# An earlier first transfer, and a last V pair cut into smaller transfers, in a transfer-bound decode kernel

## The chip, the cores and the metric

The kernel runs on one core of a Trainium2 chip. The metric is the time of one execution on the device, in microseconds (us). It is read from several executions of each kernel, alternated on the same chip. The engines carry the names of the profiles: PE does the matmuls, DVE is the vector engine, ACT the scalar engine, POOL the general-purpose one, and SP only issues transfers. L429 is line 429 of the kernel.

## The reference

One new token for each of four sequences attends over a long K/V cache; a gated MLP of the same input is mixed in.

```python
B, D, H, Sk, Dh, F = 4, 1024, 32, 8192, 128, 3584      # all bfloat16
def reference(A_x, A_k_cache, A_v_cache, A_wq, A_wo, B_x, B_w_r, B_w_gate, B_w_up, B_w_down, gate_w):
    x = A_x
    g = sigmoid((x * gate_w).sum(-1, keepdims=True))
    q = heads(x @ wq)                                    # (B, H, 1, Dh)
    p = softmax(einsum("bhqd,bhkd->bhqk", q, k_cache) * Dh ** -0.5)
    a = merge(einsum("bhqk,bhkd->bhqd", p, v_cache)) @ wo
    b = x + sigmoid(x @ w_r) * ((silu(x @ w_gate) * (x @ w_up)) @ w_down)   # B_ref runs on x, one token
    return g * a + (1 - g) * b
```

The two caches are 268 MB each and the weights bring the total to 576 MB. All of it has to be read once. (Totals and GB/s count in powers of ten; the sizes of single transfers below, 8 MB, 4 MB, 1 MB, are in units of 2^20 bytes.)

## The kernel before

All large transfers are issued by SP, in one order, into a ring of five slots of 4 MB. A "pair" is 8 MB: four heads of K or of V, filling two slots. There are 32 K pairs and 32 V pairs. A K pair goes through DVE, which transposes it piece by piece into one of two T buffers, and then through PE. A V pair goes to PE directly: 64 matmuls in 8 chunks of 8.

```python
NS = 5                                                   # ring slots
ttp = ctx.enter_context(tc.tile_pool(name="ttp", bufs=2))    # the T buffers
...
def load_pair(src, n, apart=False):
    a = slots(2)
    if a + 1 < NS and not apart:
        nc.sync.dma_start(out=flat[:, lo:lo + 2 * n], in_=src)      # 8 MB at once
        ...
def k_pair(d):
    ks = load_pair(kv_view(A_k_cache, d), RING)
    for n in range(RD):                                  # 8 pieces
        T = ttp.tile([P, CJ, 2, 32, 2], BF, name="T", tag="T")
        nc.vector.transpose(out=T..., in_=kn[...])
        for he in range(4):
            for z in range(2):
                nc.tensor.matmul(sps[:, z, :], lhsT=Z[:, he, s:s + P], rhs=T[...], ...)
        ...
def v_pair(d):
    if d < ND - 1:
        vs = load_pair(vv, RING, apart=d >= ND - 3)
    else:                                                # the last V pair
        vs = [ring[:, slots(1)] for _ in range(2)]
        nc.sync.dma_start(out=vs[0], in_=vv[:, 0:RING])              # 4 MB
        for c in range(4):                                           # 4 x 1 MB
            lo, hi = c * RING // 4, (c + 1) * RING // 4
            nc.sync.dma_start(out=vs[1][:, lo:hi], in_=vv[:, RING + lo:RING + hi])
    for c in range(RD):                                  # 8 chunks of 8 matmuls
        ...
```

The end of the program, in order: two wo blocks (1 MB each), the last V pair, the other six wo blocks (the last two in halves). The last 32 matmuls need the finished attention rows.

```python
    if (kind, d) == ("v", ND - 1):
        for g in range(2):
            wo_block(g)()
    ...
    last = [wo_block(g) for g in range(2, NWB - 2)]
    last += [wo_block(g, r, r + FR // 2) for g in (NWB - 2, NWB - 1) for r in (0, FR // 2)]
    last.pop(0)(); flush(); flush_late(); last.pop(0)()
    o_rows(GE, NWB)
    for use in last:
        use()                                            # the last 32 matmuls
```

Of the kernel before, what the change touches and what calls it, by code (L numbers as in the profile page):

```python
# [18 lines left out]
def keep_weights(nc):  # L19

    for f in nc.m.functions:
        for block in f.blocks:
            held, kept, alone = None, [], False
            for i in block.instructions:
                if i.engine == mybir.EngineType.PE:
                    if isinstance(i, mybir.InstLdweights):
                        a, y = i.ins[0], i.sync_info
                        key = (a.memref, a.offset, str(a.ap), str(a.dtype), i.tile_size, i.tile_position, i.is_transpose)
                        free = y is None or not (y.on_wait or y.on_update)
                        if free and held == key:  # L30
                            continue
                        held = key
                    elif not isinstance(i, mybir.InstMatmult) or i.ldweights is not False:
                        held = None
                kept.append(i)
            block.instructions = kept


@with_exitstack
def kernel(  # L40
# [15 lines left out]
    nc = tc.nc  # L56
# [19 lines left out]
    RING = JR * Dh  # L76
# [13 lines left out]
    mps = ctx.enter_context(tc.tile_pool(name="mps", bufs=2, space=PSUM))  # L90
    ctx.enter_context(tc.manual_schedule(engines={mybir.EngineType.PE, mybir.EngineType.DVE, mybir.EngineType.Pool}))
    nc.at_finalize(keep_weights)

    ring = const.tile([P, NS, RING], BF, name="ring")
    turn = [0]

    def slots(n):
        at = turn[0]
        turn[0] = (at + n) % NS
        return at  # L100
# [3 lines left out]
# [4 lines that stand above are left out]
            lo = a * RING  # L108
            nc.sync.dma_start(out=flat[:, lo:lo + 2 * n], in_=src)  # L109
            return [flat[:, lo:lo + n], flat[:, lo + n:lo + 2 * n]]  # L110
        halves = [ring[:, a], ring[:, (a + 1) % NS]]
        for i, half in enumerate(halves):
            nc.sync.dma_start(out=half[:, 0:n], in_=src[:, i * n:(i + 1) * n])
        return halves

    def small(shape, dtype=F32):
        return mps.tile(shape, dtype, name="small", tag="small")
# [27 lines left out]
    for he in range(4):  # L145
        half, e = divmod(he, 2)
# [170 lines left out]
    def flush():  # L317
        while pending:
            pending.pop(0)()

    def flush_late():
        while late:
            late.pop(0)()

    def heads(d):
        return divmod(d * NQ, H)

    def kv_view(cache, d):
        b, h0 = heads(d)
        return cache[b, h0:h0 + NQ].rearrange("h (r j) d -> (h r) (j d)", j=2 * JR)  # L330
# [77 lines left out]
    def v_pair(d):  # L408
        b, h0 = heads(d)
        g, t = divmod(d, GD)  # L410
        row = NM * t
        B_ = PB[g % 2]
        vv = kv_view(A_v_cache, d)
        if d < ND - 1:
            vs = load_pair(vv, RING, apart=d >= ND - 3)
        else:
            vs = [ring[:, slots(1)] for _ in range(2)]
            nc.sync.dma_start(out=vs[0], in_=vv[:, 0:RING])
            for c in range(4):
                lo, hi = c * RING // 4, (c + 1) * RING // 4  # L420
                nc.sync.dma_start(out=vs[1][:, lo:hi], in_=vv[:, RING + lo:RING + hi])
        n = 0
        for c in range(RD):
            vn = vs[c // JT]
            for z in range(2):
                for w in range(2):
                    for e in range(2):
                        j0 = CJ * (c % JT) + 16 * z + 8 * w + 4 * e
                        nc.tensor.matmul(o_ps[row:row + NM, e, :],  # L429
                                         lhsT=B_[:, RD * t + c, z, w].rearrange("p e s j -> p (e s j)"),  # L430
                                         rhs=vn[:, j0 * Dh:(j0 + 4) * Dh], start=(n == 0), stop=(n == 4 * RD - 1),
                                         skip_group_check=True)
                    n += 1
                    if n == 4:
                        flush()
                    if n == 16:
                        flush_late()
        if t < GD - 1:
            return
        o_sb = OS  # L440
        nc.scalar.activation(out=o_sb[:], in_=o_ps[:, 0, :], func=ACT.Copy, scale=mE[:, 0:1])  # L441
        nc.vector.scalar_tensor_tensor(out=o_sb[:], in0=o_ps[:, 1, :], scalar=mE[:, 1:2], in1=o_sb[:],  # L442
                                       op0=ALU.mult, op1=ALU.add)

        def finish():
            oT = small([P, GH])
            for q in range(4):
                nc.tensor.matmul(oT[:, :], lhsT=o_sb[:, q * Dh:(q + 1) * Dh],  # L448
                                 rhs=selg[:, q].rearrange("p t s -> p (t s)"), start=(q == 0), stop=(q == 3))

            def scaled():
                hg = h0 + NQ - GH
                nc.vector.scalar_tensor_tensor(out=OT[:, hg:hg + GH, b], in0=oT[:, :], scalar=sgb[:, 1, b:b + 1],
                                               in1=rinv_t[g][:], op0=ALU.mult, op1=ALU.mult)
            late.append(scaled)
        pending.append(finish)
# [12 lines left out]
    for kind, d in order:  # L469
        if kind == "k":  # L470
            k_pair(d)
            if d in side:
                side[d]()
# [3 lines that stand above are left out]
        if kind == "v":  # L477
            v_pair(d)
        if (kind, d) == ("k", ND // 2):
            add_x()  # L480
        if (kind, d) == ("v", ND - 2):
            o_rows(0, GE)
# [44 lines left out]
```

## Time and profile before

| before | value | read from |
|---|---|---|
| time, three executions | 1345.84, 1345.85, 1346.68 us | runs |
| span of the trace | 1345.3 us (execution of 1347.05 us) | page |
| share of the DMA engines, queue q1 | 99.3% | page |
| PE, DVE busy | 78%, 46% | page |
| last PE wait for V | 1.86 us | PE timeline |

These lines are from the page of the kernel before: the span, the granted TensorE clock in tenths, the DMA share in tenths and the rate in 40 slices, and the queue with packets, megabytes and share.

```profile
span 1345.3 us, 7987 instructions
...
PEclk9787988988998888899898889898899798989999
DMA  9999999999999999999999999999999999999997
GB/s 413 427 436 427 442 429 425 443 431 419 443 435 419 437 435 433 433 433 430 435 435 435 435 431 431 427 428 434 435 423 442 433 419 431 431 427 440 426 426 318
...
q1 hardware_dynamic: 13976, 575.68, 99.3%
```

The transfers fill the span: no slice but the last is below 413 GB/s. So a microsecond can be had at the two ends.

This is the end of the chain of waits of the kernel before (start, duration, what):

```profile
...
1283.83 32.50 DMA ring<-in_A_v_cache_dram
1316.38 13.11 PE o_ps L429 x60
1331.11 0.76 DVE OS L442
1331.91 1.07 PE small L448 x8
1332.98 1.82 PE acc L192 x8
1335.32 7.08 PE acc L192 x32
```

The transfer of the 4 MB half of V releases PE at 1316.38 us. From there to the end the chain is PE with its small steps on DVE (the step on ACT is among the lines left out), and no transfer.

The SP timeline of the kernel before shows issues (start, duration, what). The semaphore records of the trace count SP's landings on eight semaphores in turn, 16 increments for a transfer. From 1301.67 to 1326.34 us each of the eight issues comes 0.02 to 0.07 us after the last increment for the transfer eight issues before it. That makes an issue time a landing time:

```profile
0.80 0.40 SPq L109 DMA_DIRECT2D ring<-in_A_wq_dram  x1
...
1306.69 0.33 SPq L301 DMA_DIRECT2D ring<-in_A_wo_dram  x1
1316.40 0.33 SPq L301 DMA_DIRECT2D ring<-in_A_wo_dram  x1
1326.34 0.33 SPq L301 DMA_DIRECT2D ring<-in_A_wo_dram  x1
```

The first line is the first transfer of the program. The three others give the landings of the wo block just ahead of the last V pair (1306.69), of the 4 MB half (1316.40) and of the last 1 MB quarter of V (1326.34).

The PE timeline of the kernel before around the same place (start, duration, engine, line, operation, out<-in, elements, count, then in brackets the idle time before and what ended it):

```profile
1301.69 7.89 PE L429 MATMUL o_ps<-ring,PB 128*32 128x512 bf16 x28 [2.69 <-DMA ring<-in_A_v_cache_dram]
...
1310.90 3.62 PE L192 MATMUL acc<-ring,LT 128*4 128x512 bf16 x16 [0.32 <-DVE LT L291]
1316.38 13.11 PE L429 MATMUL o_ps<-ring,PB 128*32 128x512 bf16 x60 [1.86 <-DMA ring<-in_A_v_cache_dram]
```

The first line, the second half of the pair before the last, has 28 matmuls in 7.89 us. Here a part of it ran at half clock, and the clock record has 0.5 for 3.41 us from 1302.25 us on.

### The profile page before, as it was taken

Reading aid. Unit: us, or ns where it says so; the run is one execution under the profiler, and the core shown is the slowest. Engines: PE = TensorE matmul, PEld = TensorE weight load, DVE = VectorE, ACT = ScalarE, POOL = GpSimd, SP = SyncE. Lnnn points to the kernel's source line nnn. Section 1 sums busy time; section 2 is a strip of 40 time slices with the busy share of each in tenths; the row PEclk is TensorE's granted clock in tenths of the full one; section 3 lists DMA queues with packets and bytes.
Section 4 is the critical chain, followed back from the end, with each engine's and each line's share of the span. In section 5 each row is a group of like instructions: output and inputs, shape, how many; then the busy total and the mean of one; then the engine's idle time right before and its main releaser. Section 6 shows DMA issues by size and latency. Waiting matters only on the chain.

```text
span 1345.3 us, 7987 instructions
## 1 busy us (share of the span) xinstructions
PE 1050.1 (78%) x4536; PEld 229.2 (17%) x2348; DVE 623.1 (46%) x358; ACT 51.4 (4%) x46; POOL 59.0 (4%) x91
## 2 busy tenths in 40 slices
PE   2565977777887778878977779697779679877888
PEld 0111111112111111111211111111111112111211
DVE  4465655534445553345455456146555254556000
ACT  0000100001000100001000010001000010000000
POOL 4000100001000100001000010000000010000000
PEclk9787988988998888899898889898899798989999
DMA  9999999999999999999999999999999999999997
GB/s 413 427 436 427 442 429 425 443 431 419 443 435 419 437 435 433 433 433 430 435 435 435 435 431 431 427 428 434 435 423 442 433 419 431 431 427 440 426 426 318
DMA packets 14031, 576.20 MB, mean 428 GB/s; under 512 B 1566, under 2 KB 1574, under 8 KB 2092
## 3 DMA queue, kind: packets, MB, share of 16 engines
q1 hardware_dynamic: 13976, 575.68, 99.3%
q8 instruction: 27, 0.44, 0.1%
q14 instruction: 8, 0.07, 0.0%
q10 hardware_dynamic: 20, 0.02, 0.0%
HBM read 575.68 MB, written 0.01 MB: 428 GB/s over the span
## 4 chain that ended last, share of the span: by engine, by line
DMA 58%; PE 23%; DVE 10%; issue 8%; ACT 0%; DVEq 0%; SPq 0%; POOL 0%
DMA ring<-in_A_k_cache_dram 50%; PE S_ps L358 11%; PE o_ps L429 11%; DVE T L352 10%; DMA ring<-in_A_v_cache_dram 5%; DMA ring<-in_B_w_gate_dram 3%; PE small L448 1%; PE acc L192 1%; PE o_ps L226 0%; ACT OS L441 0%; DVEq L352 0%; DVE OS L442 0%; ACT res L495 0%; SPq L109 0%; POOL Z L335 0%
## 5 line engine op out<-in xcount | busy, mean ns | idle before, releaser
L352 DVE STREAM_TRANSPOSE T<-ring 128x2048 uint32<-128x2048 uint32 x256 | 570.6, 2282 | 501.4 <-DMA ring<-in_A_k_cache_dram 425.9
L358 PE MATMUL S_ps<-T,Z 128*128 128x512 bf16 x2048 | 536.7, 410 | 220.8 <-DVE T L352 214.8
L429 PE MATMUL o_ps<-ring,PB 128*32 128x512 bf16 x2048 | 460.5, 387 | 37.6 <-DMA ring<-in_A_v_cache_dram 37.6
L358 PEld LDWEIGHTS <-Z 128*128 128x128 bf16 x1024 | 106.2, 104 | 643.6 <-issue 635.8
L429 PEld LDWEIGHTS <-PB 128*32 128x32 bf16 x1024 | 100.7, 99 | 395.2 <-issue 373.1
L383 ACT ACTIVATE PTs<-S_ps,negm 128x1024 bf16<-128x1024 f32 x8 | 8.9, 1114 | 994.7 <-DVE negm L380 994.7
L335 POOL TENSOR_TENSOR Z<-qa,mq 128x16 bf16<-128x16 bf16 x32 | 8.3, 262 | 808.4 <-PE S_ps L358 737.3
L442 DVE SCALAR_TENSOR_TENSOR OS<-o_ps,mE,OS 128x512 f32<-128x512 f32 x8 | 6.0, 751 | 68.8 <-ACT OS L441 68.8
L394 POOL COPY PB<-PT 32x1024 bf16<-32x1024 bf16 x16 | 30.4, 1897 | 26.8 <-DVE rex L396 26.5
L392 ACT COPY PB<-PT 32x1024 bf16<-32x1024 bf16 x16 | 30.6, 1914 | 10.7 <-DVE PT L385 10.6
L291 DVE CAST LT<-small 128x64 bf16<-128x64 f32 x2 | 0.4, 224 | 46.3 <-PE small L289 46.3
L376 POOL PARTITION_ALL_REDUCE gmx<-mex x8 | 3.2, 396 | 340.6 <-DVE mex L373 340.6
L371 DVE TENSOR_REDUCE m<-S_ps 128x1 f32<-128x1024 f32 x8 | 9.8, 1225 | 15.9 <-PE S_ps L358 15.9
L402 DVE RECIPROCAL rinv<-tot 128x16 f32<-128x16 f32 x8 | 2.0, 248 | 31.1 <-POOL tot L398 31.1
L385 DVE STREAM_TRANSPOSE PT<-PTs 128x1024 bf16<-128x1024 bf16 x8 | 10.0, 1245 | 12.1 <-ACT PTs L383 12.1
L192 PE MATMUL acc<-ring,LT 128*4 128x512 bf16 x64 | 14.5, 379 | 0.7 <-DVE LT L291 0.7
L139 PE MATMUL small<-identb,x 6*128 6x6 bf16 x8 | 0.6, 196 | 15.8 <-DMA x<-in_gate_w_dram 15.8
L448 PEld LDWEIGHTS small<-selg,OS 128*128 128x128 f32 x64 | 11.8, 260 | 7.0 <-issue 4.9
L192 PE MATMUL acc<-ring,hT 128*4 128x512 bf16 x56 | 12.2, 379 | 0.0
L448 PE MATMUL small<-selg,OS 128*128 128x16 f32 x64 | 10.6, 302 | 0.9 <-DVE OS L442 0.9
L226 PE MATMUL o_ps<-ring,xw 128*4 128x512 bf16 x56 | 4.9, 481 | 7.1 <-DMA ring<-in_B_w_gate_dram 7.1
L441 ACT ACTIVATE OS<-o_ps,mE 128x512 f32<-128x512 f32 x8 | 5.5, 687 | 120.2 <-PE o_ps L429 120.2
(71 smaller groups left out, 82.2 us busy)
## 6 DMA issues: line engine op xcount, KB each, us to landing
ring<-in_A_v_cache_dram SPq DMA_DIRECT2D x15, 4096.0 KB, 30.1
ring<-in_A_k_cache_dram SPq DMA_DIRECT2D x14, 4096.0 KB, 31.8
ring<-in_B_w_gate_dram SPq DMA_DIRECT2D x1, 7168.0 KB
ring<-in_B_w_up_dram SPq DMA_DIRECT2D x1, 7168.0 KB
ring<-in_B_w_down_dram SPq DMA_DIRECT2D x2, 3584.0 KB
ring<-in_A_wo_dram SPq DMA_DIRECT2D x6, 1024.0 KB, 27.0
ring<-in_A_v_cache_dram SPq DMA_DIRECT2D x4, 1024.0 KB, 34.0
ring<-in_A_wo_dram SPq DMA_DIRECT2D x4, 512.0 KB, 17.3
```

Of the source, the lines that this page charges most:

```text
L192: nc.tensor.matmul(out_ap, lhsT=lhsT, rhs=rhs, start=start, stop=True, skip_group_check=True)
L335: nc.gpsimd.tensor_tensor(out=Z[:, :, QP - 1:QP - 1 + P].rearrange("p e (q c) -> p e q c", c=QP)[:, :, :, 0], in0=qa[:, :, h0:h0 + NQ, b], ...
L352: nc.vector.transpose(out=T[:].rearrange("p j h i e -> p (j h i e)").bitcast(U32), in_=kn[:, c * CJ * Dh:(c + 1) * CJ * Dh].bitcast(U32))
L358: nc.tensor.matmul(sps[:, z, :], lhsT=Z[:, he, s:s + P], rhs=T[:, 16 * z:16 * z + 16, half, :, e], start=(t == 0 and n == 0 and he == 0), ...
L371: nc.vector.tensor_reduce(out=m1[:], in_=sps[:].rearrange("p z n -> p (z n)"), axis=AX.X, op=ALU.max)
L383: nc.scalar.activation(out=PTs[:], in_=sps[:].rearrange("p z n -> p (z n)"), func=ACT.Exp, bias=negm[:, 0:1], scale=scale, accum_out=rs[:, ...
L385: nc.vector.transpose(out=PT[:].rearrange("p j i -> p (j i)"), in_=PTs[:])
L392: nc.scalar.copy(out=Bv[at, :, :, q, :], in_=Pv[at])
L394: nc.gpsimd.tensor_copy(out=Bv[at, :, :, q, :], in_=Pv[at])
L429: nc.tensor.matmul(o_ps[row:row + NM, e, :], lhsT=B_[:, RD * t + c, z, w].rearrange("p e s j -> p (e s j)"), rhs=vn[:, j0 * Dh:(j0 + 4) * ...
L442: nc.vector.scalar_tensor_tensor(out=o_sb[:], in0=o_ps[:, 1, :], scalar=mE[:, 1:2], in1=o_sb[:], op0=ALU.mult, op1=ALU.add)
L448: nc.tensor.matmul(oT[:, :], lhsT=o_sb[:, q * Dh:(q + 1) * Dh], rhs=selg[:, q].rearrange("p t s -> p (t s)"), start=(q == 0), stop=(q == 3))
```

## The change

The intent is twofold. First, the first transfer of the program is moved ahead of the drain with which SP enters the barrier at the start (the trace of the kernel before has 0.7 us of waiting for SP there). Second, the first 4 MB half of the last V pair arrives as two transfers of 2 MB, so that PE can start on it about 5 us sooner.

```diff
+def begin_early(nc):
+    for f in nc.m.functions:
+        head = list(f.blocks[0].instructions)
+        ...
+        at = [n for n, i in enumerate(head) if i.engine == SP and isinstance(i, mybir.InstDrain)]
+        for block in f.blocks[1:2]:
+            body = list(block.instructions)
+            n = next(n for n, i in enumerate(body) if i.engine == SP and isinstance(i, mybir.InstDMACopy))
+            i = body[n]
+            if at and not (i.sync_info is not None and i.sync_info.on_wait):
+                block.instructions = body[:n] + body[n + 1:]
+                f.blocks[0].instructions = head[:at[0]] + [i] + head[at[0]:]
...
     nc.at_finalize(keep_weights)
+    nc.at_finalize(begin_early)
...
             vs = [ring[:, slots(1)] for _ in range(2)]
-            nc.sync.dma_start(out=vs[0], in_=vv[:, 0:RING])
-            for c in range(4):
-                lo, hi = c * RING // 4, (c + 1) * RING // 4
-                nc.sync.dma_start(out=vs[1][:, lo:hi], in_=vv[:, RING + lo:RING + hi])
+            for half, cuts in ((0, 2), (1, 4)):
+                for c in range(cuts):
+                    lo, hi = c * RING // cuts, (c + 1) * RING // cuts
+                    nc.sync.dma_start(out=vs[half][:, lo:hi], in_=vv[:, half * RING + lo:half * RING + hi])
```

(`SP` stands for the full name of the engine; the first cut skips a function that has transfers in its head already.)

More of the change, by code (lines that the diff above doesn't have):

```diff
@@ L36, in keep_weights @@
             block.instructions = kept
+def begin_early(nc):
+    for f in nc.m.functions:
+        head = list(f.blocks[0].instructions)
+        if any(isinstance(i, mybir.InstDMACopy) for i in head):
+            continue
+        at = [n for n, i in enumerate(head) if i.engine == mybir.EngineType.SP and isinstance(i, mybir.InstDrain)]
+        for block in f.blocks[1:2]:
+            body = list(block.instructions)
+            n = next(n for n, i in enumerate(body) if i.engine == mybir.EngineType.SP and isinstance(i, mybir.InstDMACopy))
+            i = body[n]
+            if at and not (i.sync_info is not None and i.sync_info.on_wait):
+                block.instructions = body[:n] + body[n + 1:]
+                f.blocks[0].instructions = head[:at[0]] + [i] + head[at[0]:]
 @with_exitstack
```

## The prediction

> **What bounds the kernel now.** The transfers. The page gives queue q1 99.3% of the 16 DMA engines' span and 428 GB/s; its 40 slices show none under 413 GB/s but the last (318). PE is busy 78%, DVE 46%. A microsecond counts only at the two ends: before the first byte and after the last.
>
> **Start.** The timeline shows the first SP transfer (8 MB of wq) issued at 0.80 us; fine windows show DMA traffic from about 1.5 us. The waits of the SP queue show 0.7 us in the entry barrier. The built program has the transfer before SP's drain, so it should be issued 0.5 to 0.7 us sooner. The queue never runs dry afterwards, so all later landings move by that much. PE gets wq at 23.21 us after idling 0.56 us; nothing at the start should eat the gain.
>
> **End.** Landings can be read from the SP timeline, because each late issue waits for an older landing: the 4 MB half at 1316.40, its quarters at 1318.88, 1321.37, 1323.85, 1326.3 us. PE waits 1.86 us for the half (chain of waits: 60 matmuls from 1316.38), then runs without a real gap: 64 matmuls to 1330.2, eviction and small steps, then 32 output matmuls from 1335.32 at 0.216 us each, to 1342.2; the span ends at 1345.3.
> With the half cut in two, its first 2 MB should land near 1311.5, before PE is free (1314.4). The PE wait vanishes; PE then stays just behind the landings (last quarter 1326.3, PE reaches it at 1326.5). PE alone would finish 1.9 us earlier, near 1340.3.
> But the last half-MB of wo is nearly as late. Fine windows show the DMA share falling from 1.05 at 1335.5 to 0.06 (one engine of 16) at 1339, and that engine moving data until 1340.65. [...] one straggler sets the landing. The four matmuls that need it started at about 1341.36, so only 0.6 us of slack exists. Of the 1.9 us about 0.5 is usable; the rest becomes a new PE wait for wo, about 1.3 us.
>
> **Added cost.** One more transfer. 4 MB as one took 1316.40 - 1306.69 = 9.71 us, as four 9.94: about 0.08 us per extra transfer, on the path now. The last quarter's issue now waits for the landing of the pair before (1301.67 instead of 1291.96 us), with 9 MB still queued: harmless.
>
> **Sum.** -0.6 (start) -0.5 (end) +0.08 = -1.0 us: 1345.85 to 1344.8 us. 8 in 10: 1343.5 to 1346.1. Over 2% faster: 0.003; within: 0.994; slower: 0.003.
>
> **Signs.** Right: first SP issue at 0.0 to 0.3 us; wq matmuls about 0.6 us earlier; no wait of the V matmuls at the last pair's start; V done near 1327.6; a wait of about a microsecond before the last wo matmuls, released by a transfer; the last matmul 0.9 to 1.3 us earlier.
> Wrong at the start: same first issue, or earlier issue but unchanged first landing. Wrong at the end: last matmul 1.9 us or more earlier, or V matmuls still waiting.
>
> **What would make it wrong.** [...] the measured time starting at the first transfer, hiding the start's gain; half-rate matmuls, as at 1302 to 1305, in the last pair.

No term of the sum is cut: -0.6 -0.5 +0.08 = -1.0 us.

## The result, and the profile after

| kernel | executions | median | range | mean |
|---|---|---|---|---|
| before | 4 | 1346.26 us | 1345.84 to 1348.10 | 1346.62 |
| after | 4 | 1346.58 us | 1346.17 to 1347.79 | 1346.78 |

The ratio is 1.0001, with a 95% interval of 0.9984 to 1.0019. Ratios here are the mean time of one kernel's runs over that of the other's of the same rounds, so not quite the ratio of the medians that are quoted. The median lies above the predicted range of 1343.5 to 1346.1 us. The profiled executions differ a little: 1347.05 us before and 1346.29 us after, spans 1345.3 and 1344.6 us.

The end of the chain of waits of the changed kernel:

```profile
...
1270.46 30.53 DMA ring<-in_A_v_cache_dram
1301.06 24.63 DMA ring<-in_A_v_cache_dram
1325.75 14.89 DMA ring<-in_A_wo_dram
1340.68 1.04 PE acc L210 x4
1341.74 0.58 ACT res L513
```

The chain now ends in transfers: the last V quarter, then 14.89 us of wo, then the last four matmuls. In the kernel before it ended in PE.

The SP timeline of the changed kernel:

```profile
0.00 0.40 SPq L127 DMA_DIRECT2D ring<-in_A_wq_dram  x1
...
1305.95 0.33 SPq L319 DMA_DIRECT2D ring<-in_A_wo_dram  x1
1310.90 0.33 SPq L319 DMA_DIRECT2D ring<-in_A_wo_dram  x1
1315.80 0.33 SPq L319 DMA_DIRECT2D ring<-in_A_wo_dram  x1
1325.75 0.33 SPq L319 DMA_DIRECT2D ring<-in_A_wo_dram  x1
```

The first issue is at 0.00 us instead of 0.80 us. The first 2 MB landed at 1310.90 us, the second at 1315.80 us, the last quarter of V at 1325.75 us: 0.59 us sooner than before. The prediction's terms (0.6 us for the start less 0.08 us for the extra transfer) give 0.52 us; with the 0.80 us that the issue moved they would give 0.72 us.

The PE timeline of the changed kernel at the end:

```profile
...
1312.62 0.39 PE L447 MATMUL o_ps<-ring,PB 128*32 128x512 bf16 x1
...
1313.50 11.63 PE L447 MATMUL o_ps<-ring,PB 128*32 128x512 bf16 x52
1325.72 1.89 PE L447 MATMUL o_ps<-ring,PB 128*32 128x512 bf16 x8 [0.60 <-DMA ring<-in_A_v_cache_dram]
1328.21 1.89 PE L210 MATMUL acc<-ring,LT 128*4 128x512 bf16 x8 [0.60 <-DMA ring<-in_A_wo_dram]
...
1335.70 4.76 PE L210 MATMUL acc<-ring,LT 128*4 128x512 bf16 x20 [0.38 <-DMA ring<-in_A_wo_dram]
1340.68 1.02 PE L210 MATMUL acc<-ring,LT 128*4 128x512 bf16 x4 [0.22 <-DMA ring<-in_A_wo_dram]
```

The matmuls on the last V pair started at 1312.62 us, at first interleaved one by one with those on wo (in the lines left out), before the second 2 MB were there, as predicted. PE then caught up with the transfers and waited for them: 0.60 us, 0.38 us and 0.22 us are idle times put down to the landing of V or wo. The last four matmuls began at 1340.68 us, 0.68 us sooner than before (1341.36 us, worked out from the 32 matmuls of the chain: 1335.32 us plus 28 times 0.216 us).

### In the middle

Between the two ends something had changed that neither part of the change touches. These are the windows of the kernel before (columns: stretch, length, busy time and count of PE, weight loads, DVE, ACT, POOL, then the granted clock, DMA share and GB/s):

```profile
478.00:508.00 30.00, 22.70 (x98) 5.62 (x53) 18.78 (x10) 0.69 (x1) 0.52 (x2) 0.89 1.01 437
508.00:538.00 30.00, 23.37 (x94) 4.82 (x47) 13.19 (x6) 0.00 (x0) 0.00 (x0) 0.89 1.00 429
```

The same windows of the changed kernel:

```profile
478.00:508.00 30.00, 22.67 (x84) 5.83 (x45) 18.81 (x10) 0.69 (x1) 0.28 (x2) 0.83 1.00 424
508.00:538.00 30.00, 25.13 (x107) 5.34 (x53) 14.04 (x7) 0.00 (x0) 0.24 (x1) 0.94 0.98 422
```

From 478 to 508 us the changed kernel moved 424 GB/s instead of 437 GB/s, and its clock was 0.83 instead of 0.89. The PE timeline shows where. Before:

```profile
486.43 3.57 PE L358 MATMUL S_ps<-T,Z 128*128 128x512 bf16 x8 [5.46 <-DVE T L352]
489.80 1.00 PE L448 MATMUL small<-selg,OS 128*128 128x16 f32 x8
490.65 3.65 PE L358 MATMUL S_ps<-T,Z 128*128 128x512 bf16 x16
```

After:

```profile
486.29 3.57 PE L376 MATMUL S_ps<-T,Z 128*128 128x512 bf16 x8 [5.93 <-DVE T L370]
489.66 1.72 PE L466 MATMUL small<-selg,OS 128*128 128x16 f32 x8
491.22 5.79 PE L376 MATMUL S_ps<-T,Z 128*128 128x512 bf16 x16
```

The 16 matmuls that follow a wait took 5.79 us instead of 3.65 us. The clock record has 0.5 from 485.41 to 495.65 us, where that of the kernel before has it from 483.05 to 489.88 us. These matmuls are also what holds the two T buffers. DVE wants the next buffer and can't have it. The DVE timelines show it, that of the kernel before first, where four transposes follow each other without a wait:

```profile
492.58 8.89 DVE L352 STREAM_TRANSPOSE T<-ring 128x2048 uint32<-128x2048 uint32 x4
```

The changed kernel:

```profile
494.83 6.72 DVE L370 STREAM_TRANSPOSE T<-ring 128x2048 uint32<-128x2048 uint32 x3 [2.49 <-PE S_ps L376]
```

DVE lost 2.49 us there, so the last read of the K slot was late, so the transfer that refills the slot was issued at 497.17 us instead of 494.92 us, though the changed kernel had been ahead until then. The SP timelines, before and after:

```profile
494.92 0.33 SPq L109 DMA_DIRECT2D ring<-in_A_k_cache_dram  x1
```

```profile
497.17 0.33 SPq L127 DMA_DIRECT2D ring<-in_A_k_cache_dram  x1
```

The stream faltered by then. With the bytes of each packet spread over the packet's time, the changed kernel moved 369, 368 and 414 GB/s in the three stretches of 2 us from 498 to 504 us, where the kernel before moved 433 GB/s in each. The number of DMA engines with traffic fell to 14 or 15 of 16 from about 498.2 to 500.2 us, and 13 of the 50 packets of 64 KB that started between 495 and 503 us took 2.6 to 3.9 us, where all 57 of the kernel before took 2.4 us. Below, "runs dry" and "dry spell" mean such a dip of the rate. Why single packets got slower in it stays open.

I measured what such a spell costs from the transfer records, as the lead of the stream: the bytes moved by a time, divided by 428.6 kB per us, minus that time. Taken as an average from 460 to 490 us and again from 510 to 540 us, the lead rose by 0.49 us before (1.33 to 1.82 us) and fell by 0.19 us after (1.93 to 1.74 us). The changed kernel lost 0.68 us there, and that is as much as the start had given it: its lead over the kernel before was 0.60 us ahead of the place and -0.08 us behind it.

### The profile page after: what moved, and what is told of

It is laid out like the page before. It is cut to its first block, busy times and chain, and to the rows that moved or that the text cites. A ratio compares the mean times of both kernels' runs of the same rounds, so it can differ in the third digit from the quotient of the medians.

```text
span 1344.6 us, 7989 instructions
## 1 busy us (share of the span) xinstructions
PE 1050.9 (78%) x4536; PEld 229.7 (17%) x2348; DVE 620.5 (46%) x358; ACT 51.4 (4%) x46; POOL 57.7 (4%) x91
## 4 chain that ended last, share of the span: by engine, by line
DMA 63%; PE 19%; DVE 11%; issue 7%; another core or an unknown queue 0%; DVEq 0%; ACT 0%; SPq 0%
DMA ring<-in_A_k_cache_dram 52%; DVE T L370 11%; PE S_ps L376 11%; PE o_ps L447 8%; DMA ring<-in_A_v_cache_dram 7%; DMA ring<-in_B_w_gate_dram 3%; DMA ring<-in_A_wo_dram 1%; PE small L466 1%; DVEq L370 0%; PE acc L210 0%; ACT OS L459 0%; ACT res L513 0%; DVE rinv L420 0%; DVE OS L460 0%
## 5 line engine op out<-in xcount | busy, mean ns | idle before, releaser
L210 PE MATMUL acc<-ring,LT 128*4 128x512 bf16 x64 | 14.9, 378 | 2.0 <-DMA ring<-in_A_wo_dram 1.2
```

Source lines behind the costliest of these rows:

```text
L210: nc.tensor.matmul(out_ap, lhsT=lhsT, rhs=rhs, start=start, stop=True, skip_group_check=True)
```

## The experiments

The theories, by the letters that the expectations use:

- A: the change works as predicted, and only the scatter of executions hid it; the stream never runs dry.
- B: the gain of the start is lost in the middle of the stream.
- C (how B would come about): the stream runs dry when PE, at half clock, holds the two T buffers too long.
- D: the end of the kernel before is worse than its profile shows, because in most executions PE falls to half clock inside the last V pair.

The runs went in four batches, each on one chip, e1 to e4, e5 to e8, e9 to e12, e13 to e16, with the kernel before in each. The times of all (us):

| run | n | mean | median | standard deviation | before on the same chip, mean (n) | ratio, 95% |
|---|---|---|---|---|---|---|
| e1_both | 5 | 1346.44 | 1345.78 | 1.19 | 1347.97 (11) | 0.9987, 0.9975 to 0.9999 |
| e2_start | 6 | 1348.23 | 1347.95 | 2.1 | same | 0.9998, 0.9984 to 1.0012 |
| e3_end | 5 | 1346.46 | 1346.38 | 0.57 | same | 0.9987, 0.9975 to 0.9999 |
| e4_late | 5 | 1350.79 | 1350.16 | 1.07 | same | 1.0020, 1.0008 to 1.0031 |
| e5_t3_before | 5 | 1347.18 | 1346.61 | 1.34 | 1347.95 (9) | 0.9995, 0.9981 to 1.0008 |
| e6_t3_both | 5 | 1345.62 | 1345.62 | 0.47 | same | 0.9982, 0.9969 to 0.9996 |
| e7_before_short | 4 | 1347.93 | 1348.08 | 1.09 | same | 1.0000, 0.9986 to 1.0015 |
| e8_both_short | 4 | 1345.23 | 1345.34 | 0.58 | same | 0.9980, 0.9967 to 0.9994 |
| e9_warm_end | 5 | 1346.54 | 1346.51 | 0.38 | 1347.39 (9) | 0.9993, 0.9979 to 1.0006 |
| e10_warm_mid | 5 | 1345.93 | 1345.87 | 0.61 | same | 0.9988, 0.9975 to 1.0000 |
| e11_t3_warm_mid | 5 | 1345.57 | 1345.50 | 0.29 | same | 0.9985, 0.9973 to 0.9998 |
| e12_both_again | 5 | 1346.46 | 1346.32 | 1.42 | same | 0.9992, 0.9979 to 1.0005 |
| e13_warm_end_early | 5 | 1346.65 | 1346.45 | 0.83 | 1348.30 (9) | 0.9987, 0.9975 to 1.0000 |
| e14_t3_warm_late | 5 | 1345.82 | 1345.71 | 0.45 | same | 0.9980, 0.9966 to 0.9993 |
| e15_warm_end_again | 5 | 1346.57 | 1346.62 | 0.81 | same | 0.9987, 0.9974 to 0.9999 |
| e16_best_again | 5 | 1345.38 | 1345.59 | 0.58 | same | 0.9978, 0.9965 to 0.9990 |

### e1 to e4: the two parts apart, and a late start

e1_both is the changed kernel, unedited. e2_start and e3_end have one part each:

```diff
 # e2_start = before +
+    nc.at_finalize(begin_early)
 # e3_end = before +
+            for half, cuts in ((0, 2), (1, 4)): ...
 # e4_late = before, the first transfers made to wait for writes into their slots
+    nc.vector.memset(ring[:, 0, 0:8192], 0.0)
+    nc.vector.memset(ring[:, 2, 0:64], 0.0)
+    nc.vector.memset(ring[:, 4, 0:64], 0.0)
```

> The changed kernel again, beside the kernel before on one chip. Theory A (the change is worth about 0.7 us, the start's 0.8 us less a little at the end, and single executions scatter by more than that): mean 0.3 to 1.2 us below before, ratio 0.9991 to 0.9998, interval across 1; in the profile the last wo matmuls wait for a transfer again, and the last quarter of V lands 14.9 us before the last four matmuls. Theory B (what the start gains is lost again in the middle): the mean equals that of before to 0.3 us over all timed runs of this study, and the last landing is no earlier than before.

> Only the first transfer ahead of the entry barrier; the last V pair as before. Theory A: the first issue at 0.0 us instead of 0.8, the V matmuls of the last pair still wait about 1.9 us for their 4 MB, last matmuls end close behind the last landing; the time is 0.8 us below before (as e1 or 0.1 better), because the end of e1 is bound by the last landing anyway. If the end mattered as predicted, e1 would be 0.5 us faster than this one. Theory B: equal to before.

> Only the cut of the last V pair; the first transfer behind the barrier. Theory A: the V matmuls' 1.9 us wait goes, V is done 1.9 us sooner relative to the landing of the last quarter, but the last four matmuls wait for wo and start 14.9 us after the landing of the last quarter as before: -0.2 to +0.1 us. The prediction would have -0.4 us.

> The kernel before with a vector memset on the ring ahead of the first transfers, which delays the first issue by a time D read from the trace, about 4 us. Theory A: a shift of the first transfer passes to the end one for one, so the time is D above before, within 1 us. Theory B (a shift at the start is swallowed on the way): clearly less than D, under half of it.

By means, on one chip: before 1347.97, start alone 1348.23, end alone 1346.46, both 1346.44 us. The end is worth 1.5 to 1.8 us, three times what I had predicted, and the start nothing that these runs resolve. e4 issued its first transfer at 5.21 us, 4.41 us late, and took 2.8 us longer by the mean. That number fits neither A nor B. By the lead of the stream, e4 was 4.5 us behind the kernel before on average from 400 to 450 us and 4.0 us behind from 1250 to 1300 us, so most of a long delay at the start does reach the last transfers. (Both figures compare single profiles.) Why the mean of the times rose by less is open.

That the end is worth more than its profile said needed a reason. This is the PE timeline of e2_start, whose end is that of the kernel before:

```profile
1317.83 14.79 PE L447 MATMUL o_ps<-ring,PB 128*32 128x512 bf16 x60 [3.59 <-DMA ring<-in_A_v_cache_dram]
```

The wait is 3.59 us where the profile of before had 1.86 us, and the 60 matmuls took 14.79 us where they had taken 13.11 us. The granted clock of e2 was 0.50 from 1318 to 1320 us and 0.69 to 1322 us. The wait was shorter in the profile of before because the pair ahead of it had itself run partly at half clock there (7.89 us for 28 matmuls), so that PE came later to the wait. In e1 and e3, whose V arrives in smaller pieces, the longest wait there was 1.2 us and the clock stayed at full (1.00 in each stretch of 5 us from 1300 to 1335 us).

### e5 and e6: a third T buffer

If C holds, one more T buffer lets DVE run ahead while PE is slow. Three of them take 24 KB of each partition, and other tiles share space to make room: the input rows in the tile of the output rows, the softmax rows in a T buffer, and single buffers for the statistics.

```diff
-    ttp = ctx.enter_context(tc.tile_pool(name="ttp", bufs=2))
-    ptp = ctx.enter_context(tc.tile_pool(name="ptp", bufs=1))
-    stat = ctx.enter_context(tc.tile_pool(name="stat", bufs=2))
+    ttp = ctx.enter_context(tc.tile_pool(name="ttp", bufs=3))
+    stat = ctx.enter_context(tc.tile_pool(name="stat", bufs=1))
...
-        PTs = ptp.tile([P, 1024], BF, name="PTs", tag="PTs")
+        PP = ttp.tile([P, 2, 1024], BF, name="PP", tag="T")
+        PTs = PP[:, 0]
...
```

e5 has this with the kernel before, e6 with the changed kernel.

> The kernel before with a third transposition buffer T (paid for by letting small tiles share memory; same arithmetic). Theory C (the stream of transfers runs dry once or twice in a run, when PE at half clock holds the two T buffers and so the release of a K slot; an early start is lost there): the transposes' waits for PE shrink, the K issue near 495 us stays on time, no stretch of 5 us after 480 us falls clearly under 400 GB/s; 0.3 to 1.0 us below before. Theory A (the stream never runs dry, single executions just scatter): equal to before within 0.3 us and dips as before.

> The changed kernel with the same third buffer. Theory C: the early start is no longer lost, so this is 0.7 us or more below e5 (0.8 from the start, 0.1 to 1.8 from the end), 1.5 to 2.5 us below before, and the fastest kernel of the study; it still leads e5 by 0.6 us in the landings at mid-run. Theory A: as e1, so equal to e1 within 0.5 us. Theory B in its strong form (the lead is lost whatever the buffers): equal to e5 apart from the end.

The lead of the stream rose by 0.48 us in both over the place near 498 us: no dry spell. e6's K transfer was issued at 493.27 us, where the changed kernel had 497.17 us. The sign that the expectation named came true: in stretches of 5 us from 480 to 1300 us the rate (packets spread as above) never fell under 403 GB/s in e5 and 406 GB/s in e6. Of the 13 profiles with two buffers, 12 fall under 400 GB/s somewhere, the kernel before too (373 GB/s near 1120 us), and none of the five with three buffers does. The times: e5 is 0.77 us below the kernel before by the mean, e6 is 1.56 us below e5. A caveat: the sharing moves other things too (one addition of x goes elsewhere), so the buffer is not the only difference.

### e7 and e8: the last block of wo not loaded

To see whether the end is bound by PE or by transfers, the last 1 MB (2.5 us of transfers) is left out and the block before is used twice. The result is wrong, by little.

```diff
-    last += [wo_block(g, r, r + FR // 2) for g in (NWB - 2, NWB - 1) for r in (0, FR // 2)]
+    halves = [wo_block(NWB - 2, r, r + FR // 2) for r in (0, FR // 2)]
+    last += halves + halves
```

> The kernel before without the transfer of the last 1 MB of wo (its matmuls read the block before, so the result is wrong on purpose): 2.5 us less to transfer. If the end of the kernel before is bound by PE behind the 4 MB half: the last four matmuls still start 15.0 us after the landing of the last V quarter (16.7 where PE runs part of the last pair at half clock), and the time is that of before within 0.2 us in equal states of PE's clock. If it is bound by the transfers: 2.5 us less.

> The changed kernel without that 1 MB (wrong on purpose). The cut's gain of 1.9 us on PE is then not hidden behind the last landing: the last four matmuls start about 13.1 us after the landing of the last V quarter, with no wait for wo, and the time is about 1.9 us (more where e7 meets half clock) below e7. If the cut does nothing for PE: equal to e7.

e7 took 1347.93 us beside 1347.95 us for the kernel before: 2.5 us of transfers less at the end were worth nothing, so its end is PE's. The PE timeline of e7:

```profile
1316.15 14.80 PE L429 MATMUL o_ps<-ring,PB 128*32 128x512 bf16 x60 [3.54 <-DMA ring<-in_A_v_cache_dram]
```

Here again the 60 matmuls took 14.80 us after a wait of 3.54 us. e8 took 2.7 us less than e7, where 1.9 us or more were expected; the pair differs by the whole change and by the half clock of e7, so the time alone does not say what binds e8. Its trace does: the last four matmuls began 14.19 us after the last V landing, where they begin 14.9 us after it with the block, so the end with the cut was bound by transfers. I had expected 13.1 us and no wait: with one block less the wo landings, 2.49 us apart, still made waits, such as this one:

```profile
1327.70 1.89 PE L210 MATMUL acc<-ring,LT 128*4 128x512 bf16 x8 [0.58 <-DMA ring<-in_A_wo_dram]
```

### e9: useless matmuls in the wait ahead of the last V pair

This is the direct test of D. The end stays uncut, but PE does ten useless matmuls in the wait, so that it isn't idle for 3.5 us.

```diff
+    def warm(n):
+        spare = small([P, 512])
+        for _ in range(n):
+            nc.tensor.matmul(spare[:], lhsT=identb[:], rhs=Zt[0][...][:, 0:512], start=True, stop=True, ...)
...
         if (kind, d) == ("v", ND - 1):
             for g in range(2):
                 wo_block(g)()
+            warm(10)
```

> The kernel before with ten matmuls of no use (2.2 us) in PE's wait for the last V pair; transfers unchanged. Theory D (in most executions of the kernel before PE waits 3.5 us for the 4 MB half, is then put on half clock for 3.4 us inside the last pair, and so ends 16.7 instead of 15.0 us behind the last V quarter; the profile of before that the prediction read is one of the others): PE keeps its full clock in the last pair, the last four matmuls start 15.0 us after the landing of the last quarter, the time is 0.7 to 1.3 us below before and scatters less upwards. If half clock has nothing to do with the idle wait: equal to before, with 16.7 us in some executions.

The PE timeline of e9 (the first line is nine of the ten):

```profile
1312.24 2.10 PE L409 MATMUL small<-Z,identb 128*128 128x512 bf16 x9 [0.16 <-issue]
1315.62 13.11 PE L435 MATMUL o_ps<-ring,PB 128*32 128x512 bf16 x60 [1.27 <-DMA ring<-in_A_v_cache_dram]
```

The 60 matmuls took 13.11 us again, and the last four began 15.06 us after the last V landing, where e2, e5 and e7 took 16.7 us. The times scattered with a standard deviation of 0.38 us, none above 1347.02 us, while the kernel before reached 1349.17 us on that chip. e15_warm_end_again is the same kernel on another chip: 1346.57 us, 1.74 us below the kernel before by the mean.

> e9 again, the partner of e13 on this chip: about 1346.5 us, standard deviation under 0.6, no execution over 1347.5.

Its standard deviation was 0.81 us and one execution took 1347.65 us, both beyond what was expected; e9 and e15 together have a mean of 1346.55 us. In e15, and in e13 below, the last four matmuls began 15.44 and 15.36 us after the last V landing, a little later than in e9, but without half clock in the last pair. So useless work in the wait does for the end nearly what the cut did (e3: 1346.46 us). D is shown as far as the last pair's clock goes; the cut removes the wait and with it the slow matmuls.

### e10 and e11: useless matmuls in the middle

The same trick at the seven places where PE waits while the attention rows are finished (the profile has seven groups of them), on the changed kernel (e10) and on e6 (e11):

```diff
         # end of v_pair, once for each group of pairs
+        if d < ND - 1:
+            warm(16)
```

> The changed kernel with sixteen matmuls of no use (3.5 us) in PE's wait ahead of the first K pair of each group of heads. Theory C: the stretches at half clock there (10.2 us near 485, 953 and 1107 us in some executions) get shorter, the K issue behind them comes in time, the stream does not run dry, and the time is 0.5 to 0.9 us below e12. Theory A: equal to e12. If the added work itself hurts: above e12.

> e6 (the change and a third T buffer) with the same sixteen matmuls. Theory C: no dry stretch is left, so at or up to 0.5 us below e6's 1345.6, about 2 us below before, with the least scatter of all. If e6 has already removed them: equal to e6.

In e10 the half-clock stretch near 485 us was gone, as the PE timeline of e10 shows against the lines of before and after:

```profile
485.84 1.91 PE L376 MATMUL S_ps<-T,Z 128*128 128x512 bf16 x8 [1.80 <-DVE T L370]
487.59 0.96 PE L474 MATMUL small<-selg,OS 128*128 128x16 f32 x8
488.40 3.72 PE L376 MATMUL S_ps<-T,Z 128*128 128x512 bf16 x16
```

The eight matmuls took 1.91 us instead of 3.57 us, the K transfer was issued at 492.67 us, and the lead rose by 0.46 us over that place: no dry spell. Of the seven places, three kept a slow stretch (near 329, 797 and 953 us). Slow stretches as such are common: the changed kernel has 28 between 130 and 1290 us, e10 has 26. So with the change in place and the half clock taken away, there was no spell. This is one profile, and three of the six profiles with the early start and no cure had no spell there either; what the useless matmuls do reliably is to keep the clock up: none of the four profiles that have them has half clock near 485 us, and all 14 others do. In times, e10 is 0.53 us below e12 by the mean, with a standard error of 0.69 us. e11 has both cures: 1345.57 us with a standard deviation of 0.29 us, which is e6 (1345.62 us) again. So with the third buffer the useless matmuls added nothing that these runs resolve.

### e12 to e16: repeats, and the start alone again

```diff
 # e12_both_again = the changed kernel, unedited
 # e13_warm_end_early = e9 + begin_early
 # e14_t3_warm_late = e11 without begin_early
 # e16_best_again = e11
```

> The changed kernel once more on this chip, for the pooled comparison. With e1 the expectation is a mean 1.0 to 1.5 us below before: 1.1 from the end (1.75 us in about six of ten executions, 0.1 in the others), 0 to 0.4 from the start. If the first measurement was typical: equal to before within 0.4 us.

> e9 (before, with matmuls of no use that keep PE's clock up at the end) with the first transfer ahead of the barrier. Theory C (the lead of 0.7 us is kept until a dry stretch and mostly lost there): 0 to 0.4 us below e15 in the mean, lead over e15 in bytes before 480 us, none after 1000 us in executions that went dry. If the start passes through: 0.7 us below e15. If it costs: above.

> e11 without the early first transfer (issue at 0.8 us again). Theory C: with the stream kept from running dry the start passes through, so this is 0.6 to 0.8 us above e16, with both within 0.5 us of scatter. If the start's gain is lost for another reason: equal to e16 within 0.2 us.

> e11 again, the partner of e14: about 1345.6 us, standard deviation about 0.3, about 1.8 us below before.

e12 kept most of its lead near 498 us (+0.35 us) but ran dry near 925, 966 and 1122 us. So the place differs from execution to execution. The lead of the stream in all 18 profiles puts this in order (us; the means of the three stretches, each profile being one execution):

| profiles | 400 to 450 us | 510 to 540 us minus 460 to 490 us | 1250 to 1300 us |
|---|---|---|---|
| two T buffers, first transfer as before: before, e3, e7, e9, e15 | 0.88, 0.87, 1.01, 0.88, 0.94 | 0.49, 0.49, 0.03, 0.48, 0.46 | 7.27, 8.07, 7.44, 7.60, 7.46 |
| two T buffers, first transfer early: after, e1, e2, e8, e10, e12, e13 | 1.49, 1.68, 1.62, 1.81, 1.60, 1.59, 1.64 | -0.19, -0.55, -0.09, 0.47, 0.46, 0.35, 0.49 | 7.58, 7.45, 7.31, 8.25, 8.17, 6.46, 8.28 |
| three T buffers, first transfer as before: e5, e14 | 0.90, 0.81 | 0.48, 0.49 | 8.07, 8.01 |
| three T buffers, first transfer early: e6, e11, e16 | 1.50, 1.68, 1.59 | 0.48, 0.48, 0.49 | 8.65, 8.96, 8.91 |
| two T buffers, first transfer late: e4 | -3.58 | 0.43 | 3.29 |

The early start gives a lead of 0.7 us in every profile that has it. With two T buffers the means at 1250 to 1300 us are 7.57 us without it and 7.64 us with it: of 0.7 us, 0.1 us is left. With three T buffers they are 8.04 and 8.84 us, and the whole gain is still there. That is what B says, and the third buffer ties it to C. The table was made after all runs, its groups are of two to seven executions, and e8, e10 and e13 kept the gain with two buffers, so the early start doesn't lose it always. Nor is it the only kernel that runs dry: e7 did so near 498 us without it, and the kernel before near 1120 us.

The third buffer also removes this part of the scatter. From 400 to 450 us up to 1250 to 1300 us, the 13 profiles with two buffers gained between 4.87 us (e12) and 7.20 us (e3), 6.32 us on average; the five with three gained 7.16 to 7.31 us.

In times, the start alone was this, in pairs on one chip: e2 minus before +0.25 us, e1 minus e3 -0.02 us, e13 minus e15 +0.08 us, e16 minus e14 -0.45 us (standard errors 1.0, 0.6, 0.5 and 0.3 us). Only the last pair has the third buffer, and only there the difference has the predicted sign and comes near the size (-0.6 to -0.8 us were expected). With five executions each this does not settle it: whether the 0.8 us that the stream keeps also shortens the time by that much stays open. The lead is a mean over all traffic, and the last landing is complete only with the last of its 16 increments, which came 1.72 us after the fifteenth in the kernel before and 1.33 us in the changed one.

e16 repeated e11 at 1345.38 us, ratio 0.9978. The ten executions of that kernel have a mean of 1345.47 us and a standard deviation of 0.45 us. It beats both kernels.

### All executions together

| kernel | executions | mean | median | standard deviation |
|---|---|---|---|---|
| before | 42 | 1347.79 us | 1347.65 us | 1.36 us |
| changed (after, e1, e12) | 14 | 1346.54 us | 1346.30 us | 1.10 us |
| best (e11, e16) | 10 | 1345.47 us | 1345.55 us | 0.45 us |

The changed kernel is 1.25 us below the kernel before, with a 95% interval of 0.55 to 1.9 us (resampled executions). This pools chips; by batch the difference of the means was +0.16, -1.54 and -0.93 us, and against the 24 executions of the kernel before from these three batches alone it is -0.99 us (0.2 to 1.8 us). So the sign of the first comparison, four executions against four, was chance or the chip; I can't tell which of the two.

## Why the prediction was right or wrong

**Where the absolute number failed: "1345.85 to 1344.8 us".** The base was the median of three executions, and they happened to be at the bottom of a wide distribution: of 42 executions the lowest was 1345.84 us and the median 1347.65 us. From 1347.65 us the predicted -1.0 us would give 1346.65 us; the changed kernel's 14 executions have a median of 1346.30 us. The prediction saw a spread of 0.84 us in three runs and used it as its size. The kernel before has one of 4.7 us (1345.84 to 1350.53 us).

**The step "so all later landings move by that much" failed.** "The queue never runs dry afterwards" was read from 40 slices of 34 us each, which can't show a spell of some microseconds that costs 0.7 us. Three of the six profiles with the early start and no cure in the middle (after, e1, e2) ran dry near 498 us and a fourth, e12, later. Of the lead of 0.7 us that the start gave, 0.1 us was left at 1250 us on average with two T buffers. The term was -0.6 us; in pairs of times with two T buffers it measured +0.25, -0.02 and +0.08 us, together about +0.1 us with a standard error of 0.4 us. So the times make a full -0.6 us unlikely but do not exclude it; that the stream ran dry is read from the traces. The first issue itself moved by 0.80 us, and traffic began at 1.0 us instead of 1.8 us, so that much was right. The sign "wq matmuls about 0.6 us earlier" came out the wrong way: they began at 27.14 us instead of 23.21 us. The last of the input rows landed at 20.1 us instead of 15.7 us. It cost nothing that the trace shows, since the lead stayed.

**The step "Of the 1.9 us about 0.5 is usable" was mis-sized, twice.** In executions like the profiled one the slack was 0.1 to 0.2 us and not 0.6 us. I took the last traffic, at 1340.65 us, for the landing; the count that releases PE was complete only at 1341.13 us, and the matmuls started at 1341.36 us. The gain there was 0.1 us: the last four matmuls begin 15.02 us after the last V landing before, and 14.9 us after. The straggler was there as predicted: the last of the 16 increments of a landing came 1.29 to 1.85 us after the fifteenth after 1300 us in these two profiles. That lag is no constant. Its median over the landings after 1300 us ranges from 0.4 us (e16) to 3.9 us (e2) over the 18 profiles, so it is a part of the scatter that no experiment here holds fixed. But between the last packet and the full count lay another 0.44 us in the kernel before (1340.69 to 1341.13 us) and 0.45 us in the changed one (1340.19 to 1340.64 us), and I had left that out.

In other executions the gain is about 1.8 us (16.7 minus 14.9 us), because PE falls to half clock in the last V pair. That "half-rate matmuls, as at 1302 to 1305, in the last pair" might come stood in the prediction as something that would make it wrong, but it was not priced. It occurs in three of the five profiles that have the end as before (e2, e5, e7; not in before and e4), and in none with the cut. The matmuls of 512 columns on V start 0.216 us apart at full clock and 0.427 us apart at half clock in the traces of both kernels, and the slow stretches in their clock records last 3.41 us or a multiple of it, up to 13.65 us. Waits of 5.46 and 5.93 us in the middle (the lines at 486 us) and of 3.50 to 3.59 us in three cases of four at the end were followed by half clock. The outcome of such a wait differed between profiles, and I had read one.

The traces show more sharply which waits. Cut each trace at its clock records into windows of 3.41 us, and take the share of a window in which matmul records lie (their ends are modelled). Of the windows at full clock in the 18 profiles, all 568 with a share under 0.40 were followed by half clock, and 4 of the 5,017 with more than 0.42. So in these runs what decided was the share of matmuls in each window, not the length of the wait: ahead of the pair before the last, waits of 2.64 to 2.72 us were followed by half clock in 8 of 16 profiles. The wait for the last V pair left a share of 0.59 in the kernel before (1.86 us), and of 0.00, 0.04 and 0.34 in e2, e5 and e7 (3.52 to 3.59 us, half clock); in e4 a wait of 3.50 us was split over two windows with 0.47 and 0.51, and the clock stayed up. With the useless matmuls of e9 the share was 0.63.

**What came right.** V was done at 1327.61 us (1327.6 predicted). The wait at the start of the last V pair vanished in the profile of the changed kernel (1.21 us in e1 and e3, where PE came sooner), wo became the wait at the end, and the last matmul moved by 0.68 us, less than the predicted 0.9 to 1.3 us. The extra transfer cost 0.14 us against 0.08 us: 4 MB took 9.71 us as one transfer, 9.85 us as two (1305.95 to 1315.80 us) and 9.94 us as four.

**The sum.** A predicted difference of -1.0 us and a pooled one of -1.25 us agree by luck, because two errors cancel: the start gave about 0 instead of -0.6 us, the end -1.5 to -1.8 us in the mean (e3 minus before, e1 minus e2) instead of -0.5 us.

**Where the gain of the start goes.** One chain ties both findings: a wait of PE of several microseconds, a slow clock after it, T buffers held, a K slot read late, a refill issued late, a queue that runs dry for a moment. Each link was seen in the trace of the changed kernel: a wait of 5.93 us, half clock up to 495.65 us, 2.49 us that DVE waited for PE, the refill issued at 497.17 us, and 369 GB/s from 498 us on. Two were taken away by experiment, the clock in e10 and the buffers in e5, e6, e11, e14 and e16. The buffers are the stronger test, but not at that place, where e5 and e6 had no long stretch at half clock. Near 953 us they can be compared, with the lead taken in the same way (928 to 958 and 978 to 1008 us): it fell by 0.11 to 0.39 us in all six profiles with two buffers and a stretch of 10.2 us, and rose by 0.25 to 0.49 us in all four with three buffers and a stretch of at least 10.2 us (e6; e11, e14 and e16 have the useless matmuls too). With two buffers and a shorter stretch it lay between -0.13 and +0.39 us. A long stretch does not cost lead everywhere: near 329, 640 and 796 us the lead still rose by 0.23 to 0.45 us with two buffers and a stretch of at least 10.2 us. Nor does a spell need the early start: near 1108 us (1083 to 1113 and 1133 to 1163 us) all six profiles with two buffers and a long stretch lost 0.07 to 0.60 us, the kernel before and e15 among them, and the other twelve profiles gained 0.20 to 0.46 us.

The stretch at half clock near 485 us lasted 10.2 us in the changed kernel and 6.8 us before; its length comes in steps of 3.4 us. Of the five profiles with a stretch of 10.2 us there and two buffers, four ran dry (after, e1, e2, e7, whose lead fell short of that of the kernel before by 0.68, 1.04, 0.58 and 0.46 us over the place; e4 hardly did), and none of those with a shorter one. Three of six profiles with the early start had the long one, and two of six without (e4, e7), where nothing was done in the middle. Its length went with the phase of the windows: over the 14 profiles without useless matmuls there, the first matmul of the K pair came 0.39 to 0.45 us after the start of a stretch of 3.4 us, 0.88 to 2.14 us after that of one of 10.2 us, and 2.53 to 3.52 us after that of one of 6.8 us, with early and late starts in each group. So nothing here shows that the early start makes the long stretch likelier. What stays open is how much of the lost lead is the early start's own. Of the profiles with two buffers, those with one long stretch near 485, 953 and 1108 us gained the same lead from 400 to 450 us up to 1250 to 1300 us with the early start (6.44 and 6.64 us) and without (6.40 to 6.72 us), and those with two gained less with it (4.87 to 6.09 us) than without (6.43 and 6.87 us).

## What to carry to other kernels

Take the base of a prediction from ten or more executions before pricing half a microsecond: here a median of three lay 1.8 us below the median of 42, whose standard deviation is 1.36 us. Ask of each PE wait over about 2 us what it does in an execution where it falls whole into one window of the clock (an estimate from the 568 windows above with a share under 0.40: 0.6 of 3.41 us without matmuls was enough for half clock). This kernel was at 99.3% of its transfers, and near 498 us four profiles of its variants (after, e1, e2, e7) still lost 0.46 to 1.04 us of lead against it, to short dry spells that a page of 40 slices does not show; compare the bytes moved by a given time instead, and look for the buffer whose release waits for a slow engine. Here the cut of a late transfer or useless matmuls in its wait took away the slow end (the last four matmuls began 14.9 us after the last V landing with the cut and 15.06 us with e9's matmuls, instead of 16.7 us), one more buffer took away the dry spells (none of the five profiles falls under 400 GB/s in a stretch of 5 us), and the best kernel was 2.3 us below the kernel before by the pooled means.
